# Attention ahead of two expert layers on one core: the order of TensorE's groups, of the key steps and of the slot exponentials

## The chip, the cores and the metric

The kernel runs on one core of a Trainium2 chip. The time is that of one execution on the device, in microseconds (us); of several runs the median counts, and less is better. The inputs lie in the chip's memory and the result is written there.

## The reference

What is computed, cut to what matters (four batches of 576 tokens, 8 heads of 64, 128 random features; 2304 tokens of 512 columns for the expert layers):

```python
def phi(x):
    proj = einsum('bhsd,df->bhsf', x, w_phi)
    proj = proj - max(abs(proj), axis=-1)
    return concatenate([exp(proj), exp(-proj)], axis=-1)
q_p, k_p = phi(q), phi(k)
kv = einsum('bhsf,bhsd->bhfd', k_p, v);  z = sum(k_p, axis=2)
x = (q_p @ kv) / (q_p @ z + 1e-6)          # attention, then heads side by side
logits = x @ moe_phi                       # 32 slots: 8 experts of 4
d = softmax of logits over tokens;  c = softmax of logits over slots
slot_input = d.T @ x                       # 32 rows
slot_out   = relu(slot_input @ w1[e]) @ w2[e]   # per expert
x = c @ slot_out
# a third layer: 8 dense experts, mixed by 8 rounds of row and column scaling
```

## The kernel before

The 2304 tokens are 18 tiles of 128. The attention runs in 25 steps, i = 0 to 24 (`for i in range(NT + LAG)`). Step i adds key tile i to the sum kv of its batch, and works on query tile t = i - 7. So steps 0 to 4 hold keys alone, steps 7 to 17 keys and queries, and steps 18 to 24 queries alone. A batch of 576 tokens is four and a half tiles, so tiles 4 and 13 belong to two batches and are added twice.

Every engine works through its list in the order in which the program is written (the class `InOrder`), so this text sets the order on TensorE, VectorE, ScalarE, GpSimd and SP. The names of one step, as the profile has them:

- pk (`k_project`): 32 weight loads and products of a key tile with w_phi, into two banks of PSUM. VectorE then takes the largest absolute value mk and subtracts it (uk), once per bank; that is a shift. ScalarE makes phik by four exponentials (`k_exp`).
- kvacc (`kv_acc`): phik times the values vt, into an accumulator that fills three banks of its own (`pacc`). At the end of a batch `kv_finish` copies it out (kvs).
- pq (`q_project`): the same product for a query tile, with its shifts mq and uq. ut (`q_transpose`): uq transposed, two banks. `q_exp`: phiq, four exponentials of ScalarE out of these banks.
- num (`q_num`): phiq times kvs, two banks, copied out by ScalarE (nums); `q_divide` divides on VectorE (rd) and GpSimd, and x is there.
- xt or xl (`x_turn`): x transposed, copied by ScalarE to xT. lg (`x_logits`): xT times moe_phi, the slot logits.

Five banks of PSUM, named A to E, serve all of these but kvacc; a tile in a bank waits until the last reader of the tile before it is done. The variables n0, n1, k0, k1, q1 hold the five names and rotate each step. In the steps without keys the transposed x lies in the accumulator's banks (xl).

The softmax over tokens runs in groups of four tiles g = 0 to 3 (tiles 4g to 4g + 3), and a last group of two. Per group: `slot_max` (gm), `slot_run` (one transpose gmt, then mx, dg and the factor al), `slot_dd` (gmb, then dd, an exponential), `slot_counts` (pcs), `slot_sums` (psi, 32 x 512 products with x, added to si). `slot_norm` is the softmax over slots, in place in lg, on GpSimd for g < 3. gm, dg and dd share one buffer (tag gd). Each of these exponentials on ScalarE stands where its step is written.

The expert weights come in units of 1 MB. Some load during the attention, one unit per step, in two halves that ScalarE issues (`load_half`); the others are issued by SP when a buffer comes free (`load_units`, `load_in_x`). After the slots come the first experts (ph, po), and from about 230 us on the dense expert layer (x, y, z), which fills the rest.

Of the kernel before, what the change touches and what calls it, by code (L numbers as in the profile page):

```python
# [15 lines left out]
F = 128  # L16
# [38 lines left out]
def tile_kernel(ctx: ExitStack, tc: tile.TileContext, a):  # L55
# [102 lines left out]
    def project(pool, nm, x, t, banks):  # L158

        pss, us = [mm(f"p{nm}{t}_{j}", banks[j]) for j in range(2)], []  # L160
# [9 lines left out]
        for j in range(2):  # L170
            m = pool.tile([128, 4], F32, tag=f"m{nm}", name=f"m{nm}{t}_{j}", bufs=4)
            V.tensor_reduce(out=m, in_=h4(pss[j]), axis=AX.X, op=ALU.max, apply_absolute_value=True)
            u = pool.tile([128, 512], F32, tag=f"u{nm}", name=f"u{nm}{t}_{j}", bufs=2 if nm == "k" else 3)
            V.tensor_tensor(out=h4(u), in0=h4(pss[j]), in1=m.unsqueeze(2).to_broadcast([128, 4, F]), op=ALU.subtract)
            us.append(u)
        return us
# [4 lines left out]
    def k_project(t, banks):  # L181
        uk_t[t] = project(kp, "k", kt_t.pop(t), t, banks)

    def k_exp(t, j, c):
        if (j, c) == (0, 0):
            phik_t[t] = kp.tile([128, H, 2, F], F32, tag="phik", name=f"phik{t}")
        A.activation(out=phik_t[t][:, j::2, c, :], in_=h4(uk_t[t][j]), func=AF.Exp, scale=1.0 if c == 0 else -1.0)
        if (j, c) == (1, 1):
            uk_t.pop(t)
# [29 lines left out]
    def q_project(t, banks):  # L219
        uq_t[t] = project(qp, "q", qt_t.pop(t), t, banks)  # L220
# [74 lines left out]
    def x_turn(t, bank=None):  # L295
# [7 lines left out]
        xT = early.tile([128, KC, 128], F32, tag="xT", name=f"xT{t}", bufs=1)  # L303
# [16 lines left out]
    gm_t, dd_t, al_t = {}, {}, {}  # L320
    LAST = len(groups) - 1
# [4 lines left out]
    def slot_max(g):  # L326
# [4 lines left out]
        else:  # L331
            gm = first.tile([128, 1, NS], F32, tag="gm", name=f"gm{g}", bufs=1)
            V.tensor_reduce(out=gm.rearrange("p o j -> p (o j)"), in_=lgg.rearrange("p t j -> p j t"), axis=AX.X, op=ALU.max)
            G.tensor_copy(out=gm4, in_=gm.to_broadcast([128, 4, NS]))

    def slot_run(g, bank):
# [9 lines left out]
        if g:  # L346
            al_t[g] = al = first.tile([128, 1], F32, tag="al", name=f"al{g}", bufs=2)
            V.tensor_tensor(out=al, in0=run["m"], in1=mx, op=ALU.subtract)
            A.activation(out=al, in_=al, func=AF.Exp)
        run["m"] = mx  # L350

    def slot_dd(g, bank):
# [6 lines left out]
        A.activation(out=dd[:, 0:n], in_=dd[:, 0:n], func=AF.Exp)  # L359
        if g == LAST:  # L360
            V.tensor_scalar_mul(sels[32 * n:128], sels[32 * n:128], al_t[g][32 * n:128])
# [27 lines left out]
    def keep_busy(last, n):  # L389

        if last and n:
            pt = mm(f"busy{nbusy[0]}", None if nbusy[0] > 3 else "E")
# [8 lines left out]
    def slot_norm(g, part=None):  # L401
# [4 lines left out]
        if part != 1:  # L406
# [3 lines left out]
            A.activation(out=cc, in_=cc, func=AF.Exp)  # L410
# [13 lines left out]
    load_v(1)  # L424
    ct4 = const.tile([128, 256], F32R, name="ct4", bufs=1)
# [27 lines left out]
    for j in range(2):  # L453
        for c in range(2):
            k_exp(0, j, c)
    n0, n1, k0, k1, q1 = "CDABE"

    def slot_early(t, bank):
        for g in range(LAST):
            s = t - 4 * g  # L460
            if s == 5:
                slot_run(g, bank)
            if s == 6:
                slot_dd(g, bank)
            if s == 7:
                slot_sums(g, bank)
                if g < 3:
                    slot_norm(g, 0)
            if s == 8 and g < 3:
                slot_norm(g, 1)  # L470

    def slot_late(t, bank):
        for g in range(LAST):
            if t - 4 * g == 4:
                slot_max(g)
            if t - 4 * g == 6:
                slot_counts(g, bank)

    for i in range(NT + LAG):
        t = i - LAG  # L480
        for n in [n for n, (u, _) in enumerate(VBLOCKS) if u == i + 1]:
            place_v(n)
        if i + 3 < NT:
            load_k(i + 3)
# [9 lines left out]
        bs = [b for b, _, _ in parts_of(i)] if i < NT else []  # L494
        if t + 2 < 0:
            if len(bs) == 1:
                k_project(i + 1, "CDAB"[(i + 1) % 2 * 2:][:2])
            kv_acc(i, bs[0])
            if ((bs[0] + 1) * S - 1) // 128 == i:
                kv_finish(bs[0])  # L500
            if len(bs) > 1:
# [687 lines left out]
```

## Time and profile before

| | before |
|---|---|
| runs (us) | 1013.96, 1016.80, 1016.75; median 1016.75 |
| profiled execution: its time / its span (us) | 1015.84 / 1014.1 |
| granted clock of TensorE | 1.0 over the whole span |
| TensorE busy | 992.6 us (98%) |
| VectorE, ScalarE, GpSimd busy | 67%, 56%, 59% |
| from memory / to memory | 82.33 MB / 4.72 MB |

The span is divided by what TensorE does: attention to about 178 us, the slots' last steps to 186, the slot experts to 222, the dense experts to the end. How to read it: a row of the timeline has the start, the duration, the engine, the operation, the tile that it writes and those that it reads; a bracket at its end tells how long the engine stood idle just before, and what ended that. PEld is TensorE's weight load, which runs beside the products.

### The profile page before, as it was taken

The numbers are of one execution on the slowest core, as the hardware profiler recorded it, in microseconds if no ns is written. First come the engines' busy times: TensorE is split into PE (matmuls) and PEld (weight loads), VectorE is DVE, ScalarE is ACT, GpSimd is POOL, SyncE is SP. The second block draws the span as 40 slices with busy tenths as digits, with TensorE's granted clock in tenths as the row PEclk, the third lists the DMA queues.
The fourth block names the chain that finished last, engine by engine and source line by source line (L and its number), as shares of the span: only waits on it lengthen the run. The fifth ranks groups of instructions, "written<-read, shape, count | busy, mean of one in ns | idle before, by whom it ended". The sixth has DMA issues, their size and how long they took to land.

```text
span 1014.1 us, 27882 instructions
## 1 busy us (share of the span) xinstructions
PE 992.6 (98%) x11638; PEld 939.3 (93%) x11638; DVE 682.1 (67%) x1344; ACT 563.0 (56%) x1029; POOL 597.2 (59%) x472
## 2 busy tenths in 40 slices
PE   8899998999999999999999999999999999999998
PEld 7798887449999999999999999999999999999998
DVE  5767655357787767667667666667667667667675
ACT  5476655146566766655565556555555565455442
POOL 1122221116767776867785878578857877777443
PEclk9999999999999999999999999999999999999999
DMA  7567557983002200310031003000400130001111
GB/s 216 189 202 219 162 168 238 393 357 138 2 1 88 80 1 2 125 43 2 1 126 43 1 2 133 35 2 1 166 2 1 36 133 1 1 2 39 47 42 64
DMA packets 25486, 88.85 MB, mean 88 GB/s; under 512 B 3472, under 2 KB 6416, under 8 KB 19600
## 3 DMA queue, kind: packets, MB, share of 16 engines
q1 hardware_dynamic: 19984, 68.05, 19.1%
q10 hardware_dynamic: 5184, 18.88, 5.8%
q8 instruction: 92, 1.51, 0.6%
q14 instruction: 34, 0.28, 0.1%
q0 software_dynamic: 192, 0.13, 0.1%
HBM read 82.33 MB, written 4.72 MB: 86 GB/s over the span
## 4 chain that ended last, share of the span: by engine, by line
PE 94%; DMA 2%; ACT 1%; DVE 1%; issue 1%; POOL 0%; ACTq 0%; DVEq 0%
PE x L51 39%; PE y L51 19%; PE z L51 16%; PE num L51 4%; PE kvacc L51 3%; PE pk L51 2%; DMA moe_w<-in_moe_w 2%; PE pq L51 2%; PE ps L51 1%; PE po L51 1%; PE ut L51 1%; PE ph L51 1%; PE xl L51 1%; PE lg L51 1%; PE xt L51 1%
## 5 line engine op out<-in xcount | busy, mean ns | idle before, releaser
L51 POOL TENSOR_TENSOR hl_s<-s,hh_s 128x512 fp32r<-128x512 f32 x286 | 365.5, 1300 | 209.6 <-ACT hh_s L51 191.2
L51 PE MATMUL x<-w_t,hh_s 128*128 128x256 f32 x1152 | 205.2, 278 | 0.1
L51 ACT ACTIVATE hh_s<-s 128x512 fp32r<-128x512 f32 x287 | 175.4, 630 | 51.2 <-DVE s L51 48.6
L51 ACT ACTIVATE r<-z 128x512 f32<-128x512 f32 x143 | 85.6, 599 | 165.8 <-PE z L51 165.3
L51 PEld LDWEIGHTS x<-w_t,hh_s 128*128 128x128 f32 x1152 | 173.5, 188 | 1.1 <-ACT xo L51 0.3
L51 DVE SCALAR_TENSOR_TENSOR xo<-x,P,xo 128x256 f32<-128x256 f32 x252 | 120.8, 479 | 70.5 <-PE x L51 70.5
L51 ACT ACTIVATE hh_a<-z 128x512 fp32r<-128x512 f32 x216 | 122.1, 600 | 73.8 <-DVE s L51 72.3
L51 PE MATMUL x<-w_t,hl_s 128*128 128x256 f32 x576 | 159.1, 277 | 0.0
L51 DVE SCALAR_TENSOR_TENSOR s<-z,r 128x512 f32<-128x512 f32 x143 | 98.1, 686 | 87.4 <-ACT hh_a L51 82.7
L51 DVE SCALAR_TENSOR_TENSOR hl_a<-z,hh_a 128x512 fp32r<-128x512 f32 x216 | 147.0, 680 | 2.7 <-ACT hh_a L51 2.7
L51 PEld LDWEIGHTS x<-w_t,hl_s 128*128 128x128 f32 x576 | 108.0, 188 | 0.0
L51 PE MATMUL y<-w_t,hh_s 128*128 128x256 f32 x576 | 103.1, 278 | 0.0
L51 PE MATMUL z<-w_b,hh_a 128*128 128x256 f32 x576 | 102.5, 278 | 0.0
L51 PE MATMUL x<-w_t,hh_a 128*128 128x256 f32 x576 | 101.9, 277 | 0.0
L51 PE MATMUL y<-w_b,hh_s 128*128 128x256 f32 x576 | 101.8, 277 | 0.0
L51 PE MATMUL x<-w_b,hh_a 128*128 128x256 f32 x576 | 101.5, 276 | 0.0
L51 DVE SCALAR_TENSOR_TENSOR s<-z,s 128x512 f32<-128x512 f32 x143 | 97.7, 683 | 3.9 <-POOL hl_s L51 1.6
L51 PEld LDWEIGHTS z<-w_b,hh_a 128*128 128x128 f32 x576 | 86.7, 188 | 2.9 <-issue 2.9
L51 PEld LDWEIGHTS y<-w_t,hh_s 128*128 128x128 f32 x576 | 87.5, 188 | 0.0
L51 PEld LDWEIGHTS x<-w_t,hh_a 128*128 128x128 f32 x576 | 86.8, 188 | 0.0
L51 PEld LDWEIGHTS y<-w_b,hh_s 128*128 128x128 f32 x576 | 86.8, 188 | 0.0
L51 PEld LDWEIGHTS x<-w_b,hh_a 128*128 128x128 f32 x576 | 86.6, 188 | 0.0
(188 smaller groups left out, 1987.4 us busy)
## 6 DMA issues: line engine op xcount, KB each, us to landing
moe_w<-in_moe_w SPq DMA_DIRECT2D x45, 1024.0 KB, 6.6
moe_w<-in_moe_w ACTq DMA_DIRECT2D x36, 512.0 KB, 4.5
vs<-in_vb SPq DMA_DIRECT2D x20, 256.0 KB, 3.9
kt<-in_kT SPq DMA_DIRECT2D x18, 256.0 KB, 3.8
qt<-in_qT SPq DMA_DIRECT2D x18, 256.0 KB, 4.1
out<-xo SPq DMA_DIRECT2D x18, 128.0 KB, 1.7
out<-xo SPq DMA_DIRECT2D x9, 256.0 KB, 2.0
moe_w<-in_moe_w SPq DMA_DIRECT2D x2, 512.0 KB, 10.0
```

The source lines that it names most:

```text
L51: return lambda *args, **kwargs: self.tc.keep_in_program_order(make(*args, **kwargs))
```

## The change

It writes the attention's steps in another order.

- TensorE's groups: before num, xt, ut, pq, lg, kvacc, pk; after num, lg, kvacc, slot steps, ut, xt, pq, pk. x is transposed in its own step, and its logits come in the next.
- Keys: `k_project` runs for tile i + 2 in step i (before i + 1), key loads for i + 4 (before i + 3). The shift is a call of its own, `k_shift`, and the two halves of the key exponentials stand apart: one ahead of the query exponentials, one at the end of the step.
- Banks: pq takes the pair K0, K1, in which pk of the step before lay. num and lg take X, Q0, Q1; ut and xt take the same three behind them; pk takes X and Q0 once more.
- Slot exponentials: `exps` puts them on a list, and `run_exps` issues the list behind the copy of xT.
- Group 3: its maximum, run and dd stand in step t = 16, its counts and sums right behind the last num; before they stood behind the last xt. The last transposed x gets a buffer of its own (x6).

```diff
-        for j in range(2):
-            m = pool.tile([128, 4], F32, tag=f"m{nm}", name=f"m{nm}{t}_{j}", bufs=4)
-            V.tensor_reduce(out=m, in_=h4(pss[j]), axis=AX.X, op=ALU.max, apply_absolute_value=True)
...
+    def shift(pool, nm, t, j):
+        ps = ps_t[nm, t][j]
+        m = pool.tile([128, 4], F32, tag=f"m{nm}", name=f"m{nm}{t}_{j}", bufs=4)
+        V.tensor_reduce(out=m, in_=h4(ps), axis=AX.X, op=ALU.max, apply_absolute_value=True)
...
+    def k_shift(t, j):
+        uk_t[t, j] = shift(kp, "k", t, j)
...
+    late_exps = []
+
+    def exps(t):
+        late_exps.append(t)
+
+    def run_exps():
+        for t in late_exps:
+            A.activation(out=t, in_=t, func=AF.Exp)
+        late_exps.clear()
...
-            A.activation(out=al, in_=al, func=AF.Exp)
+            exps(al)
...
-        A.activation(out=dd[:, 0:n], in_=dd[:, 0:n], func=AF.Exp)
+        exps(dd[:, 0:n])
...
-            A.activation(out=cc, in_=cc, func=AF.Exp)
+            exps(cc)
...
+    load_k(3)
...
+    k_project(1, "AB")
...
-    n0, n1, k0, k1, q1 = "CDABE"
...
+    K0, K1, X, Q0, Q1 = "CDEAB"
...
         if 0 <= t:
-            q_num(t, 0, n0)
-        if i in uk_t:
-            k_exp(i, 0, 0)
-        if 0 <= t:
-            q_num(t, 1, n1)
-        if 0 <= t - 1:
-            x_turn(t - 1, None if q_only else n0)
...
+            q_num(t, 0, X)
+            q_num(t, 1, Q0)
+        if 0 <= t - 1 and t + 1 < NT:
+            x_logits(t - 1, Q1)
...
+        if i < NT:
+            if i + 1 < NT:
+                k_shift(i + 1, 0)
+                for c in range(2):
+                    k_exp(i + 1, 0, c)
+            if 0 <= t:
+                q_divide(t)
+            for n in place:
+                place_v(n)
+            if i + 1 < NT:
+                k_shift(i + 1, 1)
...
+            for u, c in late + [(i, b)]:
+                kv_acc(u, c)
...
+            slot_add(t, Q1, Q0)
+            slot_run_or_dd(t, Q1)
+            slot_rest(t)
+            if 0 <= t + 1:
+                for hh in range(2):
+                    q_transpose(t + 1, hh, (X, Q0)[hh])
+                    q_exp(t + 1, hh)
+            if 0 <= t:
+                x_turn(t, Q1)
+            if i in attn_units:
+                load_half(*attn_units[i], 1)
+            run_exps()
+            if ((b + 1) * S - 1) // 128 == i:
+                kv_finish(b)
+            if i + 1 < NT:
+                for c in range(2):
+                    k_exp(i + 1, 1, c)
+            if 0 <= t + 2:
+                q_project(t + 2, (K0, K1))
+                if i + 2 < NT:
+                    k_project(i + 2, (X, Q0))
+                K0, K1, X, Q0, Q1 = X, Q0, Q1, K0, K1
...
+            if t + 2 == NT:
+                slot_run(3, P0)
+            x_turn(t)
+            if t + 2 == NT:
+                slot_dd(3, P1)
+            run_exps()
...
+    slot_counts(3, P0)
+    slot_sums(3, P1)
+    x_turn(NT - 1, U1, "x6")
+    x_logits(NT - 2)
+    x_logits(NT - 1, F0)
...
-    x_turn(NT - 1)
-    slot_dd(3, "B")
-    x_logits(NT - 1)
```

How the order moves on TensorE, in a full step (x is the product of attention, hh in ut_0 and num_0 the half of the heads). Before, from the transposes to the next keys:

```order
L51 MATMUL xt_1521<-ident,x_1300 128x128 x4
L51 MATMUL ut_0_1533<-ident,uq_0_1391 128x128 x4
L51 MATMUL ut_1_1538<-ident,uq_1_1395 128x128 x4
L51 MATMUL pq_0_1552<-wbd,qt_1118 64x128 x2
L51 MATMUL pq_1_1553<-wbd,qt_1118 64x128 x2
...
L51 MATMUL lg_1578<-phi,xT_1526 64x32 x8
L51 MATMUL kvacc_1232<-vt_1291,phik_1501 64x65 x32
L51 MATMUL pk_0_1629<-wbd,kt_1114 64x128 x2
L51 MATMUL pk_1_1630<-wbd,kt_1114 64x128 x2
```

After, from the logits to the keys:

```order
L51 MATMUL lg_1548<-phi,xT_1453 64x32 x8
L51 MATMUL kvacc_1218<-vt_1391,phik_1383 64x65 x32
L51 MATMUL ut_0_1615<-ident,uq_0_1478 128x128 x4
L51 MATMUL ut_1_1624<-ident,uq_1_1482 128x128 x4
L51 MATMUL xt_1633<-ident,xx_1510 128x128 x4
L51 MATMUL pq_0_1643<-wbd,qt_1147 64x128 x2
L51 MATMUL pq_1_1644<-wbd,qt_1147 64x128 x2
...
L51 MATMUL pk_0_1669<-wbd,kt_1143 64x128 x2
L51 MATMUL pk_1_1670<-wbd,kt_1143 64x128 x2
```

lg and kvacc moved ahead of ut, xt moved behind ut, and pk now follows pq.

On ScalarE, one full step before, from the copies of num to the last query exponential:

```order
L51 COPY nums_1482<-num_0_1483 128x260
L51 ACTIVATE phik_1501<-uk_0_1464 128x4x128
L51 COPY nums_1482<-num_1_1503 128x260
L51 COPY xT_1526<-xt_1521 128x512
L51 ACTIVATE phik_1501<-uk_0_1464 128x4x128
L51 ACTIVATE phik_1501<-uk_1_1468 128x4x128 x2
L51 DMA moe_w_2_0_1531<-in_moe_w 128x1024
L51 ACTIVATE phiq_0_0_1548<-ut_0_1533 128x512
L51 ACTIVATE phiq_0_1_1549<-ut_0_1533 128x512
L51 COPY lg<-lg_1578 128x32
L51 ACTIVATE phiq_1_0_1588<-ut_1_1538 128x512
L51 ACTIVATE phiq_1_1_1589<-ut_1_1538 128x512
```

The same stretch after:

```order
L51 COPY nums_1511<-num_0_1512 128x260
L51 COPY nums_1511<-num_1_1530 128x260
L51 COPY lg<-lg_1548 128x32
L51 DMA moe_w_2_0_1558<-in_moe_w 128x1024
L51 ACTIVATE phik_1564<-uk_0_1562 128x4x128 x2
L51 ACTIVATE phiq_0_0_1620<-ut_0_1615 128x512
L51 ACTIVATE phiq_0_1_1621<-ut_0_1615 128x512
L51 ACTIVATE phiq_1_0_1629<-ut_1_1624 128x512
L51 ACTIVATE phiq_1_1_1630<-ut_1_1624 128x512
L51 COPY xT_1638<-xt_1633 128x512
L51 DMA moe_w_2_0_1558<-in_moe_w 128x1024
L51 ACTIVATE phik_1564<-uk_1_1577 128x4x128 x2
```

The four query exponentials stand together behind one pair of key exponentials, xT stands behind them, and the other pair of key exponentials behind xT.

On TensorE at the end, from num of the last tile on. Before:

```order
L51 MATMUL num_0_3472<-kvs_2780,phiq_0_0_3449 64x65 x8
L51 MATMUL num_0_3472<-kvs_2780,phiq_0_1_3450 64x65 x8
L51 MATMUL num_1_3493<-kvs_2780,phiq_1_0_3462 64x65 x8
L51 MATMUL num_1_3493<-kvs_2780,phiq_1_1_3463 64x65 x8
L51 MATMUL xl_3514<-ident,x_3383 128x128 x4
L51 MATMUL gmt_3523<-ident,gm_3467 128x128
L51 MATMUL xl_3514<-phi,xT_3519 64x32 x8
L51 MATMUL xl_3553<-ident,x_3471 128x128 x4
L51 MATMUL gmb_3560<-dg_3528,ones 128x32
L51 MATMUL xl_3553<-phi,xT_3558 64x32 x8
L51 MATMUL pcs_3576<-ones,dd_3562 32x2 x4
L51 MATMUL psi_3582<-xx_2914,dd_3562 32x512 x2
```

After:

```order
L51 MATMUL num_0_3495<-kvs_2761,phiq_0_0_3458 64x65 x8
L51 MATMUL num_0_3495<-kvs_2761,phiq_0_1_3459 64x65 x8
L51 MATMUL num_1_3516<-kvs_2761,phiq_1_0_3467 64x65 x8
L51 MATMUL num_1_3516<-kvs_2761,phiq_1_1_3468 64x65 x8
L51 MATMUL pcs_3540<-ones,dd_3489 32x2 x4
L51 MATMUL psi_3546<-xx_2922,dd_3489 32x512 x2
L51 MATMUL psi_3546<-xx_3153,dd_3489 32x512 x2
L51 MATMUL xt_3552<-ident,x_3494 128x128 x4
L51 MATMUL xl_3480<-phi,xT_3485 64x32 x8
L51 MATMUL lg_3568<-phi,xT_3557 64x32 x8
L51 MATMUL busy_3595<-ident 128x128 x5
L51 MATMUL gmt_3594<-ident,gm_3592 128x128
```

Counts and sums of group 3 (the first pcs and psi) stand ahead of the last two logits, and its gmt and gmb, in before among these rows, stand ahead of num of the last tile.

## Rows read from the trace of the kernel before

**Rows 1.** The page: busy time, share of the span, instructions of each engine

```profile
PE 992.6 (98%) x11638; PEld 939.3 (93%) x11638; DVE 682.1 (67%) x1344; ACT 563.0 (56%) x1029; POOL 597.2 (59%) x472
```

**Rows 2.** Timeline of the step t = 4, TensorE's weight loads (start, duration)

```profile
73.00 1.95 PEld L51 LDWEIGHTS num<-kvs,phiq 128*64 128x64 f32 x64 [0.17 <-issue]
...
75.01 0.42 PEld L51 LDWEIGHTS xt<-ident,x 128*128 128x128 f32 x4
...
75.40 0.90 PEld L51 LDWEIGHTS ut<-ident,uq 128*128 128x128 f32 x8
...
76.47 0.86 PEld L51 LDWEIGHTS pq<-wbd,qt 64*64 64x64 f32 x32 [0.17 <-DVE rd L51]
...
77.51 0.55 PEld L51 LDWEIGHTS lg<-phi,xT 128*64 128x64 f32 x16 [0.17 <-issue]
...
77.97 1.95 PEld L51 LDWEIGHTS kvacc<-vt,phik 128*64 128x64 f32 x64
...
79.99 0.86 PEld L51 LDWEIGHTS pk<-wbd,kt 64*64 64x64 f32 x32
...
81.02 1.95 PEld L51 LDWEIGHTS num<-kvs,phiq 128*64 128x64 f32 x64 [0.17 <-issue]
```

**Rows 3.** Timeline at t = 7 and t = 11: ScalarE's wait and TensorE's behind it

```profile
108.83 0.31 ACT L51 ACTIVATE lg<-lg 128x128 f32<-128x128 f32 x1 [5.41 <-POOL lg L51]
...
110.16 1.17 PE L51 MATMUL pk<-wbd,kt 64*64 64x128 f32 x32 [1.73 <-ACT phiq L51]
...
142.32 2.21 PE L51 MATMUL num<-kvs,phiq 128*64 128x65 f32 x64 [1.24 <-ACT phiq L51]
```

**Rows 4.** Timeline: TensorE's rows with idle time put down to issue

```profile
24.69 2.09 PE L51 MATMUL kvacc<-vt,phik 128*64 128x65 f32 x64 [0.26 <-issue]
...
33.23 1.06 PE L51 MATMUL ut<-ident,uq 128*128 128x128 f32 x8 [1.62 <-issue]
...
50.10 0.51 PE L51 MATMUL num<-kvs,phiq 128*64 128x65 f32 x10 [2.04 <-issue]
...
98.14 0.43 PE L51 MATMUL pk<-wbd,kt 64*64 64x128 f32 x3 [0.39 <-issue]
```

**Rows 5.** The chain of waits, 0 to 300 us (start, duration, engine, tile)

```profile
10.42 1.03 PE pk L51 x32
...
39.05 2.02 PE num L51 x64
...
102.05 0.99 PE psi L51 x8
...
134.99 2.02 PE num L51 x64
...
171.81 2.22 PE num L51 x64
```

**Rows 6.** Timeline: the last group's maximum on VectorE, its transpose on TensorE

```profile
179.56 0.29 DVE L51 TENSOR_TENSOR gm<-lg 128x128 f32<-128x128 f32 x1 [1.95 <-PE psi L51]
...
179.90 0.14 PEld L51 LDWEIGHTS gmt<-ident,gm 128*128 128x128 f32 x1
```

**Rows 7.** Timeline: pairs that show what follows what, and how long

```profile
34.56 1.15 ACT L51 ACTIVATE phik<-uk 128x512 f32<-128x512 f32 x2 [0.18 <-DVE uk L51]
...
35.62 2.04 ACT L51 ACTIVATE phiq<-ut 128x512 f32<-128x512 f32 x4
...
75.76 0.58 ACT L51 COPY xT<-xt 128x512 f32<-128x512 f32 x1 [0.25 <-PE xt L51]
...
77.61 0.69 DVE L51 TENSOR_REDUCE mq<-pq 128x4 f32<-128x512 f32 x1 [1.31 <-PE pq L51]
...
79.66 0.69 DVE L51 TENSOR_TENSOR uq<-pq,mq 128x512 f32<-128x512 f32 x1
```

**Rows 8.** Windows: length, busy time of PE, PEld, DVE, ACT, POOL, clock, transfers, GB/s

```profile
175.00:200.00 25.00, 22.50 (x271) 12.01 (x275) 9.69 (x46) 4.51 (x15) 3.33 (x8) 1.00 0.99 386
...
300.00:1014.00 714.00, 710.03 (x6322) 700.52 (x6321) 489.46 (x940) 395.15 (x671) 504.09 (x334) 1.00 0.13 43
```

## The prediction before the run

> **What bounds the kernel now.** I read the busy totals first: TensorE is busy for 992.6 of 1014.1 us [rows 1]. So there is nothing to win behind it; a change has to remove time in which TensorE waits, or time that it spends without streaming. From 300 us on it waits for 4.0 us in 714 [rows 8]; nearly all the rest of its idle time lies in the first 225 us, the part that this change rewrites. After that the program is the same, so what the first part wins or loses moves the end by the same amount, if the weights keep up.
>
> The second view is one step with keys and queries (t = 4, 73.0 to 81.0 us): the weight loads of TensorE, which show its seven groups back to back [rows 2]. From load to load the step is 8.02 us: num 2.01, xt and ut 1.46, pq 1.04, lg 0.46, kvacc 2.02, pk 1.03. What the reader is to see is what lies between groups. Where the tile shape changes, the next load starts late: by 0.17 us before pq, lg and num, and (77.97 + 1.95 = 79.92 against 79.99) by 0.07 us before pk. Where it does not change, from lg to kvacc, the loads run on.
>
> The waits are the third view. At t = 7 ScalarE stands 5.41 us before a slot exponential whose input GpSimd has not delivered; the query exponentials queue behind it and TensorE's pk waits 1.73 us. The same happens at t = 11, where num waits 1.24 us [rows 3]. And twice TensorE stands for 1.62 and 2.04 us with "issue", which no other engine's row explains [rows 4]; with three smaller ones (0.26 to 0.39) these are 4.6 us.
>
> The chain of waits gives the stages [rows 5]: num of t = 0 starts at 39.0, of t = 11 at 135.0, of t = 17 at 171.8; the last group's maximum reaches TensorE at 179.9 us [rows 6]. These are stages A (39.0), B (95.9), C (36.8) and D (8.1).
>
> **Full steps (stage B).** Per step the new order num, lg, kvacc, ut, xt, pq, pk drops one late load of 0.17 and one of 0.07: 8.02 - 0.24 = 7.78 us. For this the keys move a step ahead, and pk now writes the two banks that ut has just filled. Its first product into the second bank must wait for the fourth query exponential. In before a transposed tile reaches ScalarE 0.75 us after its weight load begins (xt, 75.01 to 75.76), and four exponentials take 2.04 us [rows 2, 7]. Count from the load of ut: the fourth ends at 0.75 + 2.04 = 2.79, and pk goes on at about 2.84. TensorE is there at ut and xt 1.46, pq 0.86, the first pair of pk 0.11: 2.43. So pk waits 0.4 us, and a full step comes to 8.18 us. Nothing else should hold it: VectorE's two query shifts begin 1.14 us after pq's load and take 2.74 [rows 7], one key shift 1.4 and the divide 0.4 follow, and the pair of key exponentials (1.15) is over about 1 us before the query exponentials can begin. That 1 us is the slack of the step.
>
> The Trainium skill, TensorEngine Tiling (Array Packing), Key Properties, says that a change of tiling mode drains the engine. Read as one price for every change, two of five go (before: into xt, pq, lg, pk, num; after: into ut, pq, num) and a step saves 0.34; over ten steps the time would be 1 us lower, 1008.4. The rows show 0.17 at some changes and 0.07 at another, so I keep 0.24.
>
> The Trainium skill, Perfetto Trace Analysis, Matmuls, speaks against the change: independent groups should rotate through banks, so that the copy out of one overlaps the next one's products, and pk in ut's banks does not. No row of before shows that case; the rule is one reason why rival 1 below, without the wait, has the smaller chance.
>
> Stage B, step by step from t = 0 to 10: 7.7 (no lg yet), four of 8.2, 8.4 and 8.5 with a one-column slot step (at most 0.33 each), 11.4 at t = 7 (a second kvacc of 1.95, counts and sums 1.25 by the psi row of 0.99 us [rows 5] and its neighbours), 8.2. At t = 9 there are no keys left to project and the next num waits for xT, which ScalarE copies behind the exponentials: 8.0. At t = 10, 7.3. The sum is 92.2 against 95.9. In the 95.9 are 2.4 us of "issue" and the 1.73 us wait of t = 7, which goes because the slot exponentials now stand behind the query exponentials and xT. So: -3.7 if no "issue" returns, and -1.3 if all of it does.
>
> **The start (stage A).** Up to the second pk nothing changes. From there (10.4 us) [rows 5] I add the groups: seven kvacc, seven pk, two pq, one ut at the prices above, and 0.35 for the copy of the first accumulator. That would bring num to 34.8 us. But at t = -1 there is no num and no lg to give VectorE time: pq(0) starts at 27.9, its shifts begin 1.14 later, four shift halves end at 33.2, the key exponentials 34.4, the query exponentials 36.4, then pk. num starts at 37.4 against 39.0: -1.6, with the 2.2 us of "issue" of this stage left out.
>
> **Query steps (stage C).** A step without keys is 8.02 less kvacc and pk, 5.0 us, and 5.1 with the shape changes left. Six of them are 30.4; slot steps add 2.5 (two counts and sums) and 1.1; t = 16 loses a pq (1.04) but takes in the third group's maximum, which waits for lg, and for x: +1.5. That is 34.5 against 36.8: -2.3. The waits that go are the 1.24 of t = 11 and the ones like it at t = 12, 13 and 15.
>
> **The third group's slots (stage D).** In before the last group's maximum waits 1.95 us for psi of the third group, which reads the same buffer [rows 6]. With that group two steps earlier, after num of t = 17 come counts and sums (to 3.4), xt, xT, lg (to 5.4), its copy and the maximum: 6.1 us against 8.1: -2.0. What follows to the first expert is the same, 6.6 us.
>
> **Queues moved past.** SP issues the third group's reuse of x (unit 7) about 2 us nearer to num of t = 17 than before, and units 6 and 10 as before; each transfer waits for the same buffers. But the experts' weights saturate the transfer engines from 175 us on (share 0.99, 386 GB/s) [rows 8], and TensorE now arrives 2 us nearer to them. Cost between 0 and 2.0; I take 0.9. One weight half is issued on ScalarE just ahead of the key and query exponentials; that is free as long as its buffer and its semaphore are free.
>
> **Sum.** -1.6 - 3.7 - 2.3 - 2.0 = -9.6 with no "issue" time at all. I take half of the 4.6 back, since the program is as long and its loads as many: +2.3, and +0.9 for the weights. That is -6.4 from the profiled run's 1015.84, **1009.4 us**. That run is 0.9 below the median of 1016.75 and inside the runs' spread of 2.8, which is itself about the size of the "issue" terms.
>
> **Rivals.** (1) *pk does not wait*: the exponentials keep up, or the wait hides "issue" time. Ten waits of 0.4, and 0.9 at t = 9, go: 1004.5. For it: "issue" and bank wait can overlap. Against it: the sum of 2.79 is made of rows that repeat.
> (2) *The gain is used up at the seams*: all 4.6 of "issue" return and the weights take back the whole 2.0 of stage D: 1015.84 - 9.6 + 4.6 + 2.0 = 1012.8, near the bound of no change. For it: the transfer share of 0.99.
> (3) *Slower: ScalarE becomes the bound of the full steps.* Its queue now holds, in this order, two num copies, lg, a weight half, two key exponentials, four query exponentials, xT, slot exponentials, two key exponentials; pk waits for the middle of it. If a weight half (or a late key shift on VectorE) holds that queue, pq, pk and the next shifts move with it, ten times over. The slack is 1 us; from there every microsecond counts in each of the ten steps, so 1.6 us of holding undoes the whole gain and 2.2 us gives 1009.4 + 12 = 1021.4. For it: one exponential could hold pk for 1.73 us in before. Against it: in before the same half stands behind xT without an idle row.
>
> **How the numbers follow.** Forecast 1009.4: chance 0.46. Rival 1: 0.19. Rival 2: 0.21. Rival 3: 0.14. A measurement of this kernel can tell 0.3% (3 us) from no change. The forecast and rival 1 are faster: 0.65; rival 2 lies on the bound and counts as the same: 0.21; slower 0.14. The range is 1003 to 1017: below it lies only rival 1 together with no "issue" time (0.06), above it the larger part of rival 3 (0.12).
>
> **What would show it.** In a full step of after: no late load between pq and pk or between num, lg and kvacc, an idle row before the third product of pk put down to the last phiq, and 8.2 us from num to num. ScalarE has no wait before a slot exponential. num of t = 0, 11 and 17 at about 37.4, 130 and 164 us (later by the "issue" rows met). The first expert starts near 177 instead of 186.5. It would be wrong if full steps take over 8.8 us, if TensorE waits for weights between 180 and 215 us, or if "issue" grows past 4.6 us.

## The result, and the profile after

| | before | after |
|---|---|---|
| median of the runs (us) | 1016.77 (4 runs, 1013.96 to 1017.01) | 1007.55 (4 runs, 1007.24 to 1008.91) |
| profiled execution: time / span (us) | 1015.84 / 1014.1 | 1007.74 / 1006.0 |

The ratio is 0.9918, 95% interval 0.9898 to 0.9938: faster by 0.8%, where 1009.4 us was forecast. TensorE's busy time stays nearly as it was, 989.7 us against 992.6 [rows 1]; the idle time shrank.

The starts of the stages, from the timeline of TensorE after (start, duration, engine, operation, tiles, idle before); they answer to [rows 5, 6]:

```profile
39.37 2.09 PE L51 MATMUL num<-kvs,phiq 128*64 128x65 f32 x64
...
132.87 2.09 PE L51 MATMUL num<-kvs,phiq 128*64 128x65 f32 x64
...
160.79 2.10 PE L51 MATMUL num<-kvs,phiq 128*64 128x65 f32 x64
...
167.21 2.09 PE L51 MATMUL num<-kvs,phiq 128*64 128x65 f32 x64
...
172.98 0.30 PE L51 MATMUL gmt<-ident,gm 128*128 128x128 f32 x1
...
178.63 2.80 PE L51 MATMUL ph<-moe_w,sit 128*32 128x256 f32 x48
...
223.90 1.11 PE L51 MATMUL x<-w_b,hh_a 128*128 128x256 f32 x8
```

These are num of t = 0, 11, 16 and 17, the last group's transpose, the first expert and the first dense product. In the same view of before they stand at 38.98, 134.92, 167.29, 171.81, 179.93, 186.46 and 230.41 us. So the 8.1 us between the two spans come about like this:

| stretch | before | after | difference | forecast |
|---|---|---|---|---|
| A, to num of t = 0 | 38.98 | 39.37 | +0.4 | -1.6 without "issue" |
| B, to num of t = 11 | 95.94 | 93.50 | -2.4 | -3.7 without "issue" |
| C, to num of t = 17 | 36.89 | 34.34 | -2.5 | -2.3 |
| D, to the last gmt | 8.12 | 5.77 | -2.3 | -2.0 |
| to the first expert | 6.53 | 5.65 | -0.9 | 0 |
| to the first dense product | 43.95 | 45.27 | +1.3 | +0.9 |
| to the end | 783.69 | 782.10 | -1.6 | 0 |

A full step of after, TensorE's weight loads (t = 4; answers to [rows 2]):

```profile
71.87 1.95 PEld L51 LDWEIGHTS num<-kvs,phiq 128*64 128x64 f32 x64 [0.17 <-ACT phik L51]
73.73 0.55 PEld L51 LDWEIGHTS lg<-phi,xT 128*64 128x64 f32 x16
74.20 1.95 PEld L51 LDWEIGHTS kvacc<-vt,phik 128*64 128x64 f32 x64
76.22 0.86 PEld L51 LDWEIGHTS ut<-ident,uq 128*128 128x128 f32 x8
77.04 0.47 PEld L51 LDWEIGHTS xt<-ident,xx 128*128 128x128 f32 x4
77.68 0.86 PEld L51 LDWEIGHTS pq<-wbd,qt 64*64 64x64 f32 x32 [0.17 <-issue]
78.50 0.25 PEld L51 LDWEIGHTS pk<-wbd,kt 64*64 64x64 f32 x4
79.09 0.85 PEld L51 LDWEIGHTS pk<-wbd,kt 64*64 64x64 f32 x28 [0.34 <-ACT phiq L51]
80.11 1.01 PEld L51 LDWEIGHTS num<-kvs,phiq 128*64 128x64 f32 x32 [0.17 <-ACT phik L51]
```

The late loads between num, lg and kvacc and between pq and pk are gone, and pk stops after four loads for the last query exponential; the forecast had this stop, ahead of the third product. From num to num the step takes 8.24 us, where before took 8.02. So the full steps, for which the new order was made, became longer; the gain lies elsewhere. The chain of waits of after shows the rest of the price at the far end:

```profile
170.38 12.56 DMA moe_w<-in_moe_w
...
194.64 11.11 DMA moe_w<-in_moe_w
205.77 1.05 ACT w_b L51
206.85 1.24 DVE w_b L51
208.11 1.24 DVE moe_w L51
...
212.96 1.97 PE po L51 x16
```

The last expert's po hangs on VectorE's work on the dense weights, and this on their transfer. In the timeline of TensorE these are two waits for hz, the input of po:

```profile
209.49 1.92 PE L51 MATMUL po<-moe_w,hz 128*32 128x512 f32 x16 [0.25 <-DVE hz L51]
...
212.96 1.93 PE L51 MATMUL po<-moe_w,hz 128*32 128x512 f32 x16 [0.74 <-DVE hz L51]
```

The 0.9 us gained between the last gmt and the first expert, which the forecast had at nothing, is mostly one wait of before: products that only fill time (busy) there stood in the bank of pcsum, which VectorE still had to read for rc. In after they stand in another bank, and the row is gone:

```profile
184.50 0.76 PE L51 MATMUL busy<-ident 128*128 128x128 f32 x5 [0.63 <-DVE rc L51]
```

### The profile page after: what moved, and what is told of

It reads as the page before. It is cut to its first block, busy times and chain, and to the rows that moved or that the text cites. A ratio compares the mean times of both kernels' runs of the same rounds, so it can differ in the third digit from the quotient of the medians.

```text
span 1006.0 us, 27924 instructions
## 1 busy us (share of the span) xinstructions
PE 989.7 (98%) x11638; PEld 937.4 (93%) x11638; DVE 680.2 (68%) x1345; ACT 563.2 (56%) x1029; POOL 596.9 (59%) x471
## 4 chain that ended last, share of the span: by engine, by line
PE 91%; ACT 3%; DMA 2%; DVE 2%; issue 1%; ACTq 0%; DVEq 0%
PE x L51 39%; PE y L51 20%; PE z L51 16%; PE kvacc L51 4%; PE num L51 3%; DMA moe_w<-in_moe_w 2%; ACT phiq L51 2%; PE pk L51 2%; PE ps L51 2%; PE ut L51 1%; PE po L51 1%; PE pq L51 1%; PE lg L51 0%; PE ph L51 0%; PE psi L51 0%
```

## Experiments

Where a time is that of one run, before took 1014.50 us in the same session for the doubled transposes, the key exponentials first, the slot exponentials in place and group 3 put back; 1013.25 for kvacc between ut and xt, the start and the two runs on the weights; and a median of 1016.20 for pk by bank and before traced again. Where the trace answers the question, the stages were read rather than the total. A "..." in a diff leaves out lines that don't matter for it.

**The wait of pk.** More work of TensorE was put into the stretch that the wait covers:

```diff
-        for kc in range(KC):
-            PE.transpose(ps[...], x_t[t][...], ident)
+        for _ in range(2 if 0 < t < 11 else 1):
+            for kc in range(KC):
+                PE.transpose(ps[...], x_t[t][...], ident)
```

> The kernel after, with the four transposes of x written twice into the same bank in the steps t = 1 to 10 (0.42 us more of TensorE work each, between ut and pk; the result is the same). Theory (pk waits 0.34 us for the fourth query exponential, whatever TensorE does until then): the wait takes in most of it, a full step goes from 8.24 to 8.3-8.4, num of t = 11 comes 1 to 2 us later than 132.9. Rival (the wait is no bound, the step is TensorE's own work or hides other time): full step 8.66, num of t = 11 comes 4.2 us later.

Measured: 1012.51 us. One full step (t = 3), weight loads:

```profile
67.29 0.86 PEld L51 LDWEIGHTS ut<-ident,uq 128*128 128x128 f32 x8
68.11 0.91 PEld L51 LDWEIGHTS xt<-ident,x 128*128 128x128 f32 x8
69.18 0.86 PEld L51 LDWEIGHTS pq<-wbd,qt 64*64 64x64 f32 x32 [0.17 <-issue]
70.00 1.00 PEld L51 LDWEIGHTS pk<-wbd,kt 64*64 64x64 f32 x32
71.18 0.26 PEld L51 LDWEIGHTS num<-kvs,phiq 128*64 128x64 f32 x6 [0.17 <-ACT phik L51]
```

xt takes 1.07 us in place of 0.64, the row with 0.34 is gone, and the step is 8.40: 0.43 of work cost 0.16. The wait is real, and the rival falls for the full steps. The stage as a whole grew by 5.1 us all the same. At t = 5, 3.0 us longer than in after, there is one "issue" row of 2.32 us (GpSimd stands for 1.99 us there too) where after has 0.95, and behind it the granted clock is 0.50 (1.2 GHz), so that ut takes 1.92 us in place of 1.09. At t = 10, where no pk waits, the step is 0.9 longer, twice the added work. The total can't tell the two apart, the repeated steps can.

Can the wait be had away? Once by writing pk's two banks one after the other:

```diff
-        for p in range(4):
-            for j in range(2):
+        for p, j in [(p, j) for j in range(2) for p in range(4)] if nm == "k" and t > 7 else [...]:
```

> The kernel after, with pk of the full steps written bank by bank (all products into the first bank, then all into the second) in place of by turns, so that the second bank is wanted 0.4 us later. Theory (the wait of 0.34 us is for the second bank alone): the wait goes and a full step takes 7.9 us, if products that alternate between the upper and the lower half of the rows run no better than the same products in two blocks. Rival (the two halves of the rows overlap): pk takes up to 1.7 us in place of 1.03, and a full step 8.2 to 8.7 us.

Measured: 1007.25 us, and full steps of 8.24 again. One of them:

```profile
76.75 0.86 PEld L51 LDWEIGHTS pq<-wbd,qt 64*64 64x64 f32 x32 [0.17 <-issue]
77.57 1.44 PEld L51 LDWEIGHTS pk<-wbd,kt 64*64 64x64 f32 x32
79.18 0.43 PEld L51 LDWEIGHTS num<-kvs,phiq 128*64 128x64 f32 x12 [0.17 <-ACT phik L51]
```

The wait is gone, as the theory had it, but 32 loads of which 16 go to one half of the rows and then 16 to the other take 1.44 us, where by turns they take 0.86. So the step is the rival's: from pk to num it is 1.61 us in either form.

And once by giving the exponentials more time, with kvacc between ut and xt:

```diff
-            for u, c in late + [(i, b)]:
-                kv_acc(u, c)
...
             if 0 <= t:
+                add_keys()
                 x_turn(t, Q1)
```

> The kernel after, with kvacc between ut and xt in the steps from t = 0 on: the query exponentials are done long before pk, and two changes of tile shape are added. Theory (the bank wait is 0.34 us a step, a change of shape 0.07 to 0.17): the wait before pk goes and a full step takes 8.04 to 8.24 us against 8.24. If a change of shape cost more than 0.17, the step would be longer than 8.24.

Measured: 1010.60 us (with a stretch at a granted clock of 0.50 at num of t = 17; see the last section); steps of 8.23 and 8.24 at t = 3 and 4. From pk to num it is 1.09 us in place of 1.61, so the wait is gone. But ut now starts 0.15 us later behind lg than kvacc did, kvacc 0.20 later behind ut than xt did, and lg, for a reason that no row names, 0.23 later behind num. That is the upper end of what was expected: the changes of shape and lg cost what the wait had cost. At t = 10 the step took 8.91 in place of 7.44.

**ScalarE's slack.** All key exponentials ahead of the query exponentials:

```diff
                 k_shift(i + 1, 1)
+                for c in range(2 if 0 <= t else 0):
+                    k_exp(i + 1, 1, c)
```

> The kernel after, with all four key exponentials ahead of the query exponentials on ScalarE in the steps from t = 0 on (the second pair, 1.15 us, stands behind the copy of xT in after). Theory (pk hangs on ScalarE, which has 0.99 us of room ahead of the query exponentials): the second pair begins when the second key shift is done, about when ut starts, and pushes the query exponentials by about 0.5 us; the wait of pk grows from 0.34 to 0.5-0.9 and num of t = 11 comes 2 to 5 us later. Rival (ScalarE is no bound of the step): num of t = 11 within 0.5 us.

Measured: 1007.88 us; full steps of 8.50, and pk's idle row is 0.61 in place of 0.34:

```profile
71.85 0.85 PEld L51 LDWEIGHTS pk<-wbd,kt 64*64 64x64 f32 x28 [0.61 <-ACT phiq L51]
```

The stretch from num of t = 0 to t = 11 takes 94.60 us against 93.50, though it holds no "issue" row and after's holds 0.95; without those it is 2.1 us longer, at the lower end of the theory. So 1.15 us of earlier work on ScalarE costs 0.26 a step, because pk's delay also delays the next ut. ScalarE does bound the step, but the rival that went slower, with its full price in each step, was too steep.

**The slot exponentials.** Back where each slot step is written:

```diff
     def exps(t):
-        late_exps.append(t)
+        A.activation(out=t, in_=t, func=AF.Exp)
```

> The kernel after, with each slot exponential issued on ScalarE where its slot step is written, ahead of the query exponentials. Theory of the prediction (a slot exponential that waits for GpSimd holds the query exponentials): ScalarE waits before lg at t = 7 and t = 11 again, num of t = 11 comes 1.5 to 2 us later and num of t = 17 3 to 5 us later. Rival (in the new order GpSimd is done before ut, because kvacc and the slot steps now stand ahead of it): less than 0.5 us over the whole attention.

Measured: 1010.16 us; the first dense product comes 2.3 us later. But 1.5 us had gone to the clock ahead of it: at num of t = 17 the granted clock is 0.50 (1.2 GHz), and the last stage takes 7.31 us in place of 5.77:

```profile
168.88 3.33 PE L51 MATMUL num<-kvs,phiq 128*64 128x65 f32 x64
```

So this run is read from its steps. ScalarE at t = 7:

```profile
107.34 0.31 ACT L51 ACTIVATE lg<-lg 128x128 f32<-128x128 f32 x1 [3.86 <-POOL lg L51]
107.56 0.58 ACT L51 ACTIVATE phiq<-ut 128x512 f32<-128x512 f32 x1
```

In after the same exponential stands behind the query exponentials and xT, without a wait:

```profile
108.63 0.35 ACT L51 ACTIVATE lg<-lg 128x128 f32<-128x128 f32 x1
```

So the wait of [rows 3] is back. The step t = 7 takes 13.48 us against 11.17: 1.0 more from ut to num, 0.8 of "issue". t = 9 is 0.5 longer. But t = 11 to 16 take 34.48 against 34.34. At t = 11 ScalarE waits for GpSimd again (2.64 us before lg), but TensorE does not pay for it. The theory holds at t = 7 alone; TensorE's waits at t = 11 to 15 had gone with the order of the groups, not with the place of the exponentials.

**The start.** In the one step t = -1 other banks and another order on ScalarE:

```diff
-                for c in range(2):
+                for c in range(2 if t + 1 else 0):
                     k_exp(i + 1, 0, c)
...
+            if t + 1 == 0:
+                for c in range(2):
+                    k_exp(i + 1, 0, c)
+                K1, Q1 = Q1, K1
```

> The kernel after, with two things changed in the one step t = -1: the second pq takes the free bank Q1 and one bank of pk(7) in place of both banks of pk(7), and the first pair of key exponentials of tile 7 stands behind the query exponentials. Theory (the start lost its gain because pq waits 1.00 us for the key shift, and pk then 0.54 us for query exponentials that stand behind a key pair): num of t = 0 starts 1 to 1.7 us earlier, counted without idle rows put down to issue, and the rest follows unchanged. Rival (VectorE's shifts set the start in any order of banks): num of t = 0 within 0.3 us.

Measured: 1003.79 us; num of t = 0 at 36.60. What stood there in after, on TensorE:

```profile
29.75 1.10 PE L51 MATMUL pq<-wbd,qt 64*64 64x128 f32 x32
...
35.21 0.44 PE L51 MATMUL pq<-wbd,qt 64*64 64x128 f32 x4 [0.36 <-PE ut L51]
36.65 0.98 PE L51 MATMUL pq<-wbd,qt 64*64 64x128 f32 x26 [1.00 <-DVE uk L51]
...
38.35 1.09 PE L51 MATMUL pk<-wbd,kt 64*64 64x128 f32 x28 [0.54 <-ACT phiq L51]
```

on ScalarE, which sets when this pk goes on:

```profile
35.20 1.15 ACT L51 ACTIVATE phik<-uk 128x512 f32<-128x512 f32 x2 [5.02 <-DVE uk L51]
36.26 2.04 ACT L51 ACTIVATE phiq<-ut 128x512 f32<-128x512 f32 x4
```

and the same groups of TensorE with the edit:

```profile
34.23 1.10 PE L51 MATMUL pq<-wbd,qt 64*64 64x128 f32 x32 [0.37 <-PE ut L51]
35.12 1.55 PE L51 MATMUL pk<-wbd,kt 64*64 64x128 f32 x32
36.60 1.62 PE L51 MATMUL num<-kvs,phiq 128*64 128x65 f32 x48
```

From ut to num it is 3.83 us against 5.61: 1.8 us, so the theory holds. It repeats: from the first pq to num it is 7.76 to 7.83 us in the three traces with this edit and 9.61 or 9.62 in the nine of the new order without it. The rest of the 2.8 us lies ahead of ut, where starts differ from execution to execution (num of t = 0 at 38.15 to 39.37 in those nine). What the two changes are worth apart was not run. By the rows the bank alone would gain nothing, since pk would still stand until the query exponentials end at 38.30.

**Group 3.** Its steps back behind the last num:

```diff
-            if t + 2 == NT:
-                slot_run(3, P0)
             x_turn(t)
-            if t + 2 == NT:
-                slot_dd(3, P1)
...
-    slot_counts(3, P0)
-    slot_sums(3, P1)
+    slot_run(3, P0)
+    x_logits(NT - 2)
     x_turn(NT - 1, U1, "x6")
-    x_logits(NT - 2)
+    slot_dd(3, P1)
...
     slot_max(4)
+    slot_counts(3, P0)
+    slot_sums(3, P1)
```

> The kernel after, with the slot steps of group 3 back behind the last num (gmt ahead of the last-but-one logits, gmb ahead of the last, counts and sums behind them). Theory of the prediction: the last stage gets back its wait of gm for psi and takes about 8 us (5.77 in after), but the step t = 16 loses its waits for gm and gmb (1.75 us), so the first expert starts only 0.5 to 1.5 us later than 178.6. Rival (the move is worth what the last stage alone shows): 2.3 us or more later.

Measured: 1006.66 us. The last stage grows from 5.77 to 6.86 us, and t = 16 shrinks from 6.42 to 5.07, because these rows of after go:

```profile
165.71 0.33 PE L51 MATMUL gmt<-ident,gm 128*128 128x128 f32 x1 [1.35 <-DVE gm L51]
...
166.88 0.40 PE L51 MATMUL gmb<-dg,ones 32*128 32x32 f32 x2 [0.40 <-DVE al L51]
```

From num of t = 16 the first expert is as far as in after (17.67 and 17.84 us): the move gained nothing there. Both expectations missed: I had the last stage back at 8 us. Even behind the last num, group 3 does better in the new order of the tail. And the first dense product came 61.86 us after num of t = 16, against 63.11.

**The weights.** Two runs on the stretch from the first expert to the first dense product. The first takes VectorE's subtractions out of hz's way:

```diff
         if e == 5:
             w_begin(0)
             w_hi(0, 0)
-            w_lo(0, 0, V)
-            w_sum(0, 0, V)
         if e == 6:
-            w_lo(0, 3, V)
-            w_sum(0, 1, V)
+            w_lo(0, 0, V)
+            w_sum(0, 0, V)
         if e == 7:
+            w_lo(0, 3, V)
+            w_sum(0, 1, V)
```

> The kernel after, with the dense layer's first weight subtractions on VectorE one expert later, so that they stand behind hz of experts 6 and 7. Theory (TensorE's waits of 0.25 and 0.74 us for hz come from these subtractions, whose weights landed late): both waits go and the last po starts 1 us earlier; the first dense product comes up to 1 us earlier if the subtractions still end in time, or up to 2.5 us later if they don't. Rival (hz itself is late): the waits stay.

Measured: 1008.89 us. Both waits for hz went, but ScalarE's copy behind the last po then waited behind a cast whose input came late, and TensorE with it:

```profile
215.30 1.21 PE L51 MATMUL p_sot<-sel,os 128*128 128x128 f32 x8 [1.88 <-ACT os L51]
```

The first dense product came 47.17 us after the first expert, against 45.27, but only 0.5 of these 1.9 us are the edit's: p_sot begins 37.23 us after the first expert, against 36.74. The other 1.4 are the clock. Behind the wait of 1.88 us the granted clock is 0.50 (1.2 GHz), and ps takes 1.94 us where it takes 1.07 in after:

```profile
217.29 1.94 PE L51 MATMUL ps<-moe_w,sot 128*32 128x256 f32 x16
```

So taking the two waits away gained nothing, and they look like the front of a chain that has to run anyhow. The second run loads less:

```diff
-            load_units(wb, 30, 31)
+            load_units(wb, 30)
+            unit_t[units[31]] = unit_t[units[30]]
```

> The kernel after, with one expert weight unit of 1 MB not loaded (the last half of the last expert's second matrix is taken from the unit before, so the result of that expert is another). Theory (from num of t = 17 on the experts run at the pace of the weights, which arrive at about 420 GB/s): the first cast of dense weights on ScalarE comes up to 2.5 us earlier than 205.8, the waits for hz go, and the first dense product comes about 1 us earlier than 223.9. Rival (the transfers are no bound there): cast and product within 0.3 us.

Measured: the cast came 37.07 us after num of t = 17, against 38.56, and the first dense product 44.00 us after the first expert, against 45.27; hz waits at neither of the two places. So one unit less gave back what the stretch had lost, which fits a stretch that runs at the pace of the weights. But a single run can't give the size: with all units loaded, ten traces of the new order (without the run on hz) take 44.19 to 45.54 us from the first expert to the first dense product. What sets this run apart is that each of the ten waits for hz late in the stretch at least once (0.19 to 0.74 us), and this one doesn't. (The total, 1006.76, holds a slow end; see below.)

**What belongs to one execution.** The kernel before, traced again:

> The kernel before, once more, for a second trace of it. In the first one the last 58 us (five rows of 24 products at 2.83 us where 65 others take 2.72) were 1.6 us longer than in after, and idle rows put down to issue came to 4.6 us. Theory (both belong to one execution, not to the kernel): other sums this time, the steps t = 2 to 4 at 8.0 us again, num of t = 7 to 8 at 12.8 us again. Rival (they belong to the kernel before): the same five rows at the end and 4 to 5 us of issue at the same places.

Measured: 1014.01 us. The steps repeat: t = 3 and 4 take 8.03 and 8.02, t = 7 takes 12.75. Of the "issue" rows [rows 4] two repeat to the digit, 1.62 ahead of the first ut and 0.26 ahead of a kvacc; the one of 2.04 is 0.91 now, and the sum is 3.1. The slow end doesn't repeat.

What repeats has a cause in the program. The first ut of before goes into a bank of the key projection, and it starts, at 33.23, 0.1 us after VectorE has read that bank:

```profile
32.44 0.69 DVE L51 TENSOR_TENSOR uk<-pk,mk 128x512 f32<-128x512 f32 x1
```

In the second trace the two stand at 33.11 and 33.00. The row of 0.26 starts 0.1 us after ScalarE has copied out the first accumulator, and so does one row of 0.25 to 0.85 in each of the 14 traces. Both are waits for a bank that the profile puts down to "issue"; a forecast can count on them.

**A version that beats both.** The edits of the start and of group 3 together:

> The two edits that gained alone, together: group 3's slot steps back behind the last num, and the step t = -1 with the free bank and the query exponentials first. Theory (the first gives 1.7 us at the first dense product, the second 2 to 3 us at num of t = 0, and both come ahead of the same weights): about 1002 to 1003 us. Rival (the weights from 160 us on take back what comes earlier than in the better of the two): no better than the 1003.8 us of the second alone.

Measured: 1004.72 us, median of 4 runs (1004.21 to 1005.83), ratio to before 0.9890 (0.9865 to 0.9915). That is short of the theory; whether it is better than the start alone, a single run can't tell. So the start alone was timed as well:

> The kernel of the start experiment again, timed: after with the step t = -1 changed alone, group 3's slot steps where after has them. Theory (what is gained behind num of t = 16 does not reach the end, because the weights run from there on; group 3's place is then worth nothing): within 1 us of the 1004.7 us that the same start has with group 3 put back. Rival (group 3's waits at t = 16 cost 1.75 us that reach the end): 1006 us or more.

Measured: 1006.01 us, median of 6 runs (1005.03 to 1007.71), ratio 0.9906 (0.9885 to 0.9926). The median misses the theory's bound and just reaches the rival's; the two versions lie 1.3 us apart, and their runs overlap. All six runs lie above the 1003.79 of the single run of the same kernel, so one total says little at this size. That group 3's move costs up to 1 us is likely from the two traces with it put back (the first dense product 61.86 and 62.24 us after num of t = 16; 62.55 to 63.39 in five with it moved, and 63.70 to 63.87 in three that hold a stretch at the lower clock there), but not settled. Both versions have medians below after's 1007.55, and the runs of the first don't reach after's fastest.

## Why the prediction was right, point by point

- **Full steps: right.** 8.24 us against 8.18. Taking out xt's 0.43 from the 8.40 of the first experiment leaves 7.97 with 0.14 of pk's slowing (1.00 against 0.86 us) still in it: about 7.8 without a wait, where 7.78 was worked out; so the wait is worth some 0.4, as forecast. Its row shows only 0.34, since the four loads ahead of it are spread as well (0.25 us for four, where 32 take 0.86).
- The Trainium skill, TensorEngine Tiling (Array Packing), Key Properties, says that a change of mode drains the engine. The trace agrees that it costs, but not at one price: 0.17 ahead of pq and num, and 74.20 + 1.95 against 76.22, 0.07, ahead of ut.
- The Trainium skill, Perfetto Trace Analysis, Matmuls, wants independent groups to rotate through banks. pk in the banks of ut shows why: 0.34 idle in every full step.
- **Stage B: right but for "issue".** 93.50 with 0.95 of "issue", so 92.55 without, against 92.2. But also before falls to 93.5 without its 2.4. The gain of the order itself is 1 us. It sits at t = 6 and 7 (9.34, with 0.39 of "issue", to 8.57, and 12.76 to 11.17), and part of it is spent again: 0.5 at t = 0 and 0.2 in each full step.
- **The start: wrong.** num came at 39.4 where 37.4 was worked out. From the first pq to num the chain held: its shifts begin 1.14 us after it, the key exponentials end at 36.3, the query exponentials at 38.3, and num comes 9.62 us after pq, against 9.5. (The "four shift halves" of the prediction are three by their times, two of q and one of k; three is what the trace shows.) The step that failed is the sum of groups up to that pq, 27.9: it starts at 29.75. Of these 1.85 us 0.71 are "issue" rows (0.40 and 0.31), 0.4 a stretched pk, and 0.2 the later pk from which the sum counts (10.66 in place of 10.4); the rest are pieces of 0.1 to 0.2. Part of it is no chance: the copy of the first accumulator was put at 0.35, but where no other stop came before it TensorE stands for it 0.72 to 0.85 us (eleven traces), and the earliest trace of this order, with no other "issue" row there, still has pq at 28.53. The wait of 1.00 us in pq of t = 1, whose banks VectorE empties late, was left out too, but by the rows it cost nothing by itself: pk behind it still stood 0.54 us for the query exponentials. The experiment on the start shortened a chain that had been forecast rightly.
- **Query steps: right in size** (-2.5, forecast -2.3), and wrong in part of the reason: with the slot exponentials back in place the stretch is only 0.14 longer, so TensorE's waits of t = 11 to 15 went with the order.
- **Stage D: right where it was measured, and without use.** -2.3 there (forecast -2.0) and -0.9 to the first expert, but +1.9 at t = 16 (6.42 against 4.52), and the weights took 1.3. What was won by num of t = 16, 167.29 to 160.79, is 6.50 us; at the first dense product it is 6.51. In these two traces nothing that was won behind it arrived.
- **Weights: right** (1.3 against 0.9, between the bounds), though the ten traces of the new order spread from 0.2 to 1.6. From SP's first weight row in this stretch (165.55 and 159.48) to the first cast it is 46.4 us in before and 46.3 in after. One sign of being wrong was met without the forecast failing: TensorE does wait between 180 and 215 us for work that hangs on weights, 0.25 and 0.74 us.
- **"Issue": right by chance.** 2.3 was put back; after's trace has 1.9, the others 0.7 to 3.5. The reason was wrong as well: of before's 4.6 us 1.62 were no chance but the wait of the first ut for a bank, which the new order doesn't have, and 0.26 the wait for the copied accumulator.
- **Rivals.** The first, no wait of pk, falls to the row with 0.34. The second came half true: the weights took 1.3 of its 2.0, but only 1.9 of 4.6 us of "issue" came back. The third needed ScalarE to hold pk; the experiment on the slack did that on purpose and met 0.26 a step.
- **The total: its nearness is partly luck.** Without "issue" the start came 1.0 us later than forecast and stage B 0.4, and the first expert came 0.9 earlier for a wait that no step had named. The rest, 1.6 us of the 8.1, is before's slow end, which no step foresaw and which the change didn't make. That takes the difference of the traces to 6.5, the forecast's 6.4. The medians differ by 9.2. For the other 2.7 us the clock is a likely cause, not shown by a trace of those runs: of 18 later timed runs of before the four with a mean granted clock of 1.000 take 1012.84 to 1014.94 us, the 14 with 0.997 or 0.998 take 1013.91 to 1020.63, eight of them 1016.2 or more; of after's four runs one has less than 1.000 (1007.35).

## What to carry to other kernels

An order that saves idle time between groups is worth only what the engine behind it can follow: here saving 0.24 us a step ran into a 0.4 us wait for a bank, and two ways round it cost just as much. Before a step is moved up ahead of a stage that runs at the pace of its transfers, look which event starts those transfers: of the time won after that event little reached the end here. When a stage misses, lay its path beside the one that was worked out, piece by piece, before naming the longest wait as the cause: the wait of 1.00 us here lay beside the path, and the time had been lost ahead of it. A path that was forecast rightly can still be shortened, as the start was by 1.8 us. And trace a kernel twice before its unexplained idle rows are called noise: the rows that repeat are waits.

## What the runs showed of the hardware

The same products can run 4% longer for a stretch with no idle row and no lower granted clock. From the chains of before and of after, 24 products near the end:

```profile
966.90 2.83 PE x L51 x24
977.74 2.83 PE x L51 x24
```

```profile
960.27 2.72 PE x L51 x24
970.75 2.72 PE x L51 x24
```

In before this lasts from 956 us to the end, at a granted clock of 1.00 (2.4 GHz). In 13 of the 14 traces one group of 24 at this place takes 2.79 to 2.89 us. In nine of them the next groups take 2.72 again, and four stay slow to the end: the first trace of before (the second doesn't), the new version, the start alone when timed, and the run with one unit less. The stretch from the first dense product to the end is 1.6 to 1.8 us longer with it than in after. What makes it is open. The weight loads of 32 products that alternate between the two halves of the rows take 0.86 us, those that go half by half 1.44.

The granted clock of TensorE was at its lower level, 0.50 (1.2 GHz), for a few microseconds in five of the 14 traces: the doubled transposes (twice), the slot exponentials in place, kvacc between ut and xt, the subtractions moved behind hz, and the second trace of before. The step or stage that held one was 1.4 to 1.6 us longer for it. TensorE had stood 2.32 us just before one of them and 1.88 before another. But in three traces the clock fell behind the waits of 1.35 and 0.40 us at t = 16, which after has as well, at a clock of 1.00.

Most "issue" rows, of up to 2.3 us, come and go between executions of nearly the same program, all ahead of 105 us. What ends them has a mark in the traces. One queue of the profile's page is called "instruction" (in before):

```profile
q8 instruction: 92, 1.51, 0.6%
```

These are blocks of 16 KB. Of the "issue" rows of TensorE's products in the 14 traces 22 are not the two waits for a bank named above. All 22 (0.2 to 2.32 us) end 1.25 to 1.61 us after such a block has landed; for the six longest (0.79 to 2.32 us) the block had started 5.5 to 7.7 us after the one before it, where most come 3.5 to 5 us apart. That TensorE stood for want of instructions fits this, but no run tests it.
